# Batch 3 of a fused attention and SwiGLU kernel: its exponentials are summed on GpSimd, and its denominators are made behind the value round

## The chip, the core and the metric

The kernel runs on one core of a Trainium2 chip. The time is that of the device for one execution, in microseconds (us), as the median of three runs. In the profile PE is TensorE's matrix multiply, PEld TensorE's weight load (which runs beside it), DVE is VectorE, ACT is ScalarE, POOL is GpSimd and SP is SyncE. L258 means line 258 of the kernel.

## What is computed

There are 8 batches of 8 heads with 576 positions and 64 columns each. Attention goes through 32 memory slots: the exponentials of `phi` weigh keys and values into 32 rows for each head, and the queries attend to those rows. A SwiGLU block with 512 columns in, 1536 inside and 512 out follows.

```python
a = np.exp(phi - max(phi, axis=2))                  # (B, H, S, 32)
a = a / (np.sum(a, axis=2) + 1e-09)                 # the denominators
k_m = np.einsum('bhsm,bhsd->bhmd', a, k)
v_m = np.einsum('bhsm,bhsd->bhmd', a, v)
attn = softmax(q @ k_m^T / sqrt(64))
x = (attn @ v_m) as (B*S, 512)
g = x @ w_gate
out = (g / (1 + exp(-g)) * (x @ w_val)) @ w_out
```

The sum over the 576 positions in the second line is what the change is about.

## The kernel before

**Batches.** Batches 0 and 1 are handled together at the start. From batch 2 on, one pass of the loop at L996 handles batch b: scores, exponentials, normalisation, then "the gates" of batch b. The gates are 24 slots (`gv_slot`, L545). In each slot TensorE makes a gate product of one slot and the value product of the slot before (four matmuls of 288 columns), ScalarE takes the gate through Silu (L532), and VectorE multiplies it by the value product (L538). `spread` (L852) puts other work between the slots by keys: slot s has the key s + 0.5, and the two items of the next batch's keys and values stand at the keys 7 and 9, so behind the seventh and behind the ninth slot. Each engine runs its instructions in the order in which this program issues them.

**Keys and values of the next batch.** `kv_items(b + 1, beside)` (L292) gives two items. The first, `run_sums`, makes

- the denominators (`kv_denominators`, L239): products of 128 columns of exponentials with `ones2`, two columns wide (L258);
- the sums for keys and values (`kv_sum`, L222), 72 small matmuls (L230) into two PSUM banks;
- the reciprocal of the denominators on VectorE (L262), and `kv_norm` (L268), four VectorE instructions (L266) that scale the sums by it into `t_bkv`;
- `beside()`: the value round of the current batch's third chunk of columns (`u_item(b, 2, "aava")`), which is 16 matmuls (L472) into four banks and four copies out of them, of which the first, second and fourth are ScalarE's (L492) and the third VectorE's (L496), and then up to two units of output products of the batch before (L727). In the gates of batch 2 no such units are left.

The second item, `kv_T` (L278), transposes `t_bkv`. For batches 2 and 3 this is done on TensorE, by three products with the identity (L288), and VectorE copies the result (L289). For batches above 3 it is a DMA transpose on SyncE's queue (L284).

**Two orders of `run_sums`.** Where `phi_sum(b + 1)` has run, the exponentials of the nine row groups have been added up on GpSimd (L212), and the sum is held as two bf16 parts (L218, L219); then the batch is in `esums`, the denominators take two products, and they stand behind `beside()`, as do the reciprocal and `kv_norm`. Otherwise, with `beside` given, the denominators take nine products into a bank of their own (`p_S`) and stand first, with their reciprocal; `kv_norm` follows the sums, and `beside()` comes last. Before the change batches 4, 6 and 7 take the first way, batches 3 and 5 the second. Batch 2 is made with nothing beside it.

**GpSimd.** Its queue holds the Strassen-like sums of the hidden activations (`chunk_done`, L586, on the lines L603 and L560), the issue of the loads (L94 to L108), and `phi_sum`. That one starts with `wait_for(atts[b - 1, 1])`, a copy of one element that waits for the second normalisation (L452) of the current batch.

**PSUM.** Eight banks are handed out in the order in which they were given back in the program (`bank` and `done`, L75 to L84).

Of the kernel before, what the change touches and what calls it, by code (L numbers as in the profile page):

```python
# [14 lines left out]
def kernel(  # L15
# [98 lines left out]
    def load_qT(b):  # L114

        qTs[b] = att.tile([128, NS, 128], BF16, tag="qT", name="t_qT")
        nc.sync.dma_start_transpose(out=qTs[b], in_=qs[b])
# [52 lines left out]
    def phi_exp(b):  # L170
        t = att.tile([128, JK, NP, M], BF16, tag="ephi", name="t_ephi")
        nc.scalar.activation(
            out=t.rearrange("p j i m -> p i j m"),
            in_=phis.pop(b).rearrange("p i (j m) -> p i j m", m=M),
            func=AF.Exp,
        )
        ephis[b] = t
# [114 lines left out]
    def kv_items(b, beside=None):  # L292


        def run_sums():
            o = 2 * D
            behind = b in esums
            own = beside and not behind
            if own:
                d = bank([128, NG], FP32, "p_S")  # L300
                kv_denominators(b, d)
                kv_reciprocal(b, d)
                done(d)
            p = [bank([128, CH], FP32, f"p_kv{g}") for g in range(NG)]
            if not (own or behind):
                kv_denominators(b, p[0][:, o:o + NG])
            kv_sum(b, p, (0, 1))
            if behind:
                beside()
                kv_denominators(b, p[0][:, o:o + NG])  # L310
            if not own:
                kv_reciprocal(b, p[0][:, o:o + NG])
            kv_norm(b, p)
            if beside and not behind:
                beside()

        return [run_sums, lambda: kv_T(b)]
# [74 lines left out]
    def scores(b, g):  # L392
        p = gv_banks()
        for i in range(NP):
            for r in range(2):
                nc.tensor.matmul(  # L396
                    p[r][32 * i:32 * i + 32, 0:HALF],
                    lhsT=kTs[b][64 * r:64 * r + 64, g, 32 * i:32 * i + 32],
                    rhs=q_of(b, i, g, r),
                    start=True,  # L400
                    stop=True,
                    tile_position=(64 * r, 32 * i),
                )
        e = att.tile([128, 2, HALF], BF16, tag=f"E{g}", name="t_E")
        for r in range(2):
            scale = rks[b][:, g:g + 1] if b in rks else sm_scale
            nc.scalar.activation(
                out=e[:, r].rearrange("p (c s) -> p c s", c=NC),
                in_=p[r][:, 0:HALF].rearrange("p (s c) -> p c s", c=NC),
                func=AF.Exp,  # L410
                scale=scale,
            )
        done(*p)
        es[b, g] = e
# [35 lines left out]
    def norm(b, g):  # L450
        a = att.tile([128, 2, HALF], BF16, tag=f"A{g}", name="t_A")
        nc.vector.tensor_tensor(out=a, in0=es.pop((b, g)), in1=lzs.pop((b, g)), op=ALU.mult)  # L452
        atts[b, g] = a
# [108 lines left out]
    def weight_sums(c, part=(0, 1, 2, 3)):  # L562

        if 0 not in part:
            t = Ts[c]
            for n in part:
                x, y = Ts[c, n]
                subtract(nc.vector, t[:, n], x, y)
            return
        home = dict(tag=f"mphi{c}", bufs=1) if c < 2 else dict(tag="T2", bufs=1)  # L570
        t = att.tile([128, 4, 2, DM // 2], BF16, name="t_T", **home)
        w = WOc[c].rearrange("p (m e) f -> p e m f", e=2)
        h = DM // 2
        B11, B12, B21, B22 = (w[:, e, :, h * n:h * n + h] for e in range(2) for n in range(2))
        Ts[c] = t
        for n, xy in enumerate(((B12, B11), (B22, t[:, 0]), (B22, B12), (B21, t[:, 1]))):
            Ts[c, n] = xy
            if n in part:
                subtract(nc.vector, t[:, n], *xy)
# [62 lines left out]
    def wait_for(x):  # L642

        t = att.tile([1, 1], BF16, tag="mark", bufs=1, name="t_mark")
        nc.gpsimd.tensor_copy(out=t, in_=x)
# [183 lines left out]
    def q_items(b, evac):  # L829
        return [lambda n=n: q_T(b, n, evac[n]) for n in range(3)]  # L830
# [9 lines left out]
    def u_three(b):  # L840

        evac = "avavav" if b in (3, 5) else "avaava"
        u_round(b, (((0,), 0, (0, 1)), ((1,), 0, (0, 1)), ((0,), 1, (0, 1))), evac)

    def u_values(b):

        u_round(b, (((1,), 1, (0, 1)),), "aa")
    def run(items):
        for x in items:
            x()  # L850
# [10 lines left out]
    def exp_tables():  # L861
        nc.scalar.preload_act_table_set("natural_log_exp_and_others")
# [111 lines left out]
    def take(n):  # L974
        nonlocal backlog
        n = max(0, min(n, len(backlog)))
        part, backlog = backlog[:n], backlog[n:]
        return part
# [3 lines left out]
    def loads(b):  # L982

        if b < B:
            load_q(b)
            load_phi(b, nc.gpsimd)
            load_k(b)
            load_v(b)

    def run_late():  # L990
        run(late)
        late.clear()
# [3 lines left out]
    for b in range(2, B):  # L996
        last = b + 1 == B
        exp_tables()
        if b == 2:
            load_qT(3)  # L1000
            phi_exp(2)
            (zero, ops0), (one, ops1) = products(0, ("c11",)), products(1, ("p1", "c11"))
            kv, q2 = kv_items(2), q_items(2, "aaa")
            run(zero[:6])
            sums = {n: f for n, f in zip(((1, 1), (0, 2), (1, 2)), late)}
            late.clear()
            sums[0, 2]()
            weight_sums(0)
            weight_sums(1)
            run(zero[6:12] + one[:6] + kv[:1] + q2[:2])  # L1010
            weight_sums(2, (0, 1))
            run(zero[12:16] + zero[18:22] + kv[1:] + q2[2:] + zero[16:18] + zero[22:24])
            weight_sums(2, (2, 3))
            ops0["c11"]()
            ops1["p1"]()
            wait_for(Ts[2][0:1, 3, 0, 0:1])
            for part in ((0, 1), (3,), (2,)):
                for c in (1, 2):
                    sums[1, c](part)
            loads(4)  # L1020
            backlog = one[6:12] + zero[36:] + one[12:36]
            ops = ops1
        else:
            run(take(6))
        for g in range(NG):
            scores(b, g)
        if b > 2:
            ops["p1"]()
            u_values(b)
        else:  # L1030
            run(zero[24:36] + take(6))
        run(take(6))
        z_inv_v(b, 0)
        ops["c11"]()
        run(take(6))
        if not last:
            phi_exp(b + 1)
        z_inv_v(b, 1)
        if b > 2:
            norm(b, 0)  # L1040
            norm(b, 1)
        run(take(6))
        run_late()
        if b == 4:
            wait_for(atts[4, 1][0:1, 0, 0:1])
            quad_sums(0)
        nc.scalar.preload_act_table_set("silu_and_others")
        run(take(6))
        if b == 2:
            norm(2, 0)  # L1050
        run(take(6))
        if b == 2:
            norm(2, 1)
            u_three(2)
            run(one[36:])
        g = gv_slots(b)
        quad = []
        if b == 4:
            quad = products(b, (), 0)[0]
        if last:  # L1060
            rest, rest_ops = products(b, (), 1)
            backlog += rest[:12]
        beside = 0 if last else 2 if quad else min(4, len(backlog))
        outs = [lambda: run(take(1)) for _ in range(len(backlog) - beside)]
        streams = [(g, 0, 24), (quad[:12], 0, 3), (quad[12:], 12, 18.5)]
        streams += [(outs, 4, 7 if quad else 24)]
        if b == 2:
            streams += [([lambda: u_values(2)], 2.5, 3)]
        if last:
            streams += [([u_item(b, 2)], 5, 6)]  # L1070
        if not last:
            if b > 2:
                load_qT(b + 1)
            if b > 2 and b != 4:
                phi_sum(b + 1)
            streams += [
                (kv_items(b + 1, lambda: (u_item(b, 2, "aava")(), run(take(2)))), KV, KV + 4),
                ([lambda: (u_three(b + 1), run(take(2)))], 19, 20),
            ]
        spread(*streams)  # L1080
        flush_mul()
        units, ops = products(b, ("p1", "c11"))
        backlog += units
# [34 lines left out]
```

## Time and profile before

| what | value |
|---|---|
| median of three runs | 233.5 us (233.14 to 233.53) |
| span of the profiled execution, first to last instruction | 231.4 us |
| TensorE busy | 221.6 us, 96% |
| VectorE, ScalarE, GpSimd busy | 185.1 us (80%), 171.7 us (74%), 140.8 us (61%) |
| gates of batch 2, first to last gate product | 76.35 to 91.1 us |
| sums of batch 3 (L230) | from 80.28 us |
| transposes of batch 3 (L288) | from 82.44 us |
| granted TensorE clock, mean | 0.997 |

The page and the trace are of one execution. Its own total time is not recorded, so what lies around the span in it is not known; 2.1 us lie between the span and the median of the other runs (233.5 - 231.4). A timeline line gives the start, the duration of the merged group, the engine, the source line, the operation, what is written and read, and how many instructions are merged. For TensorE the durations of a group contain the pipeline's latency, so the distance from the start of one group to the start of the next is the time that it occupies the engine.

### The profile page before, as it was taken

To read this page: it belongs to the slowest core of one execution; us is meant where nothing else is said; L and a number is where in the kernel's file an instruction comes from. 1 tells how busy PE (TensorE), PEld (TensorE's weight loads), DVE (VectorE), ACT (ScalarE), POOL (GpSimd) and SP (SyncE) were. 2 spreads that over 40 slices of the span, in tenths; PEclk is the share of its full clock that TensorE was granted. 3 is DMA by queue.
4 is the path that set the end of the run, shared out by engine and by line. 5 is a ranking of instruction groups with operands and counts; after the bars stand their busy time and mean duration, and the time that the engine had idled before them with its cause. 6 is when DMAs were issued, how large, how long until landed. Compare 5 with 4: busy or idle time off the path is not lost.

```text
span 231.4 us, 7210 instructions
## 1 busy us (share of the span) xinstructions
PE 221.6 (96%) x2825; PEld 169.8 (73%) x2825; DVE 185.1 (80%) x423; ACT 171.7 (74%) x365; POOL 140.8 (61%) x190
## 2 busy tenths in 40 slices
PE   6987799999999999999999999999999999999993
PEld 2544476778887777878788787887788778878882
DVE  4245789999966799989997668998999899977732
ACT  2777898988447989968896658978898789677310
POOL 8422427998199049765977689464845394039291
PEclk9999999999999999999999999999999999999998
DMA  6999999999996992999299946994014502202125
GB/s 214 210 211 206 199 207 207 221 245 268 205 225 175 256 256 49 223 204 184 71 223 191 226 134 115 252 236 89 28 65 114 104 0 95 91 10 84 31 85 160
DMA packets 36674, 36.84 MB, mean 159 GB/s; under 512 B 14624, under 2 KB 31008, under 8 KB 36640
## 3 DMA queue, kind: packets, MB, share of 16 engines
q0 software_dynamic: 16272, 22.42, 52.5%
q1 hardware_dynamic: 19600, 13.18, 22.9%
q10 hardware_dynamic: 768, 0.79, 1.1%
q8 instruction: 22, 0.36, 0.6%
q14 instruction: 12, 0.10, 0.1%
HBM read 42.47 MB, written 9.44 MB: 224 GB/s over the span
## 4 chain that ended last, share of the span: by engine, by line
PE 86%; DMA 9%; POOL 2%; ACT 1%; issue 0%; DVE 0%; POOLq 0%
PE p_g L515 21%; PE p_os L727 21%; PE p_v L515 20%; PE p_oc L727 10%; DMA W<-in_moe_w_val_dram 9%; PE p_oa L727 5%; PE p_u L472 5%; PE p_kv L230 2%; PE p_g L396 1%; POOL t_kv L99 1%; POOL t_kv L103 1%; PE p_q L383 0%; POOL t_q L108 0%; ACT t_qT L337 0%; POOL W L138 0%
## 5 line engine op out<-in xcount | busy, mean ns | idle before, releaser
L538 DVE TENSOR_TENSOR t_h<-t_sg,p_v 128x288 bf16<-128x288 bf16 x192 | 81.8, 451 | 14.1 <-PE p_v L515 7.0
L515 PEld LDWEIGHTS <-t_U 128*128 128x128 bf16 x768 | 73.9, 98 | 21.2 <-issue 3.5
L532 ACT ACTIVATE t_sg<-p_g 128x288 bf16<-128x288 f32 x192 | 73.3, 424 | 17.1 <-PE p_g L515 11.4
L515 PE MATMUL p_g<-t_A,t_U 128*128 128x288 bf16 x384 | 77.0, 286 | 0.0
L515 PE MATMUL p_v<-t_A,t_U 128*128 128x288 bf16 x384 | 77.0, 286 | 0.0
L727 PEld LDWEIGHTS <-t_S 128*128 128x128 bf16 x384 | 37.5, 98 | 4.5 <-issue 0.2
L603 POOL TENSOR_TENSOR t_S<-t_h 128x512 bf16<-128x512 bf16 x17 | 19.7, 1157 | 32.7 <-DVE t_h L538 31.2
L727 PEld LDWEIGHTS <-t_h 128*128 128x128 bf16 x288 | 27.1, 98 | 8.6 <-issue 5.0
L492 ACT CAST t_U<-p_u 128x512 bf16<-128x512 f32 x51 | 27.0, 605 | 6.6 <-PE p_u L472 6.6
L727 PE MATMUL p_os<-t_T,t_S 128*128 128x256 bf16 x192 | 23.7, 273 | 0.0
L560 POOL TENSOR_TENSOR t_S<-t_S,t_h 128x512 bf16<-128x512 bf16 x17 | 19.6, 1156 | 1.3
L560 POOL TENSOR_TENSOR t_S<-t_h 128x512 bf16<-128x512 bf16 x16 | 18.4, 1152 | 0.0
L560 POOL TENSOR_TENSOR t_S<-t_h,t_S 128x512 bf16<-128x512 bf16 x16 | 18.4, 1152 | 0.0
L472 PE MATMUL p_u<-W,t_kT 64*32 64x512 bf16 (+1 forms) x416 | 15.3, 363 | 1.2 <-DMA W<-in_moe_w_gate_dram 0.6
L496 DVE CAST t_U<-p_u 128x512 bf16<-128x512 f32 x21 | 13.6, 683 | 1.9 <-PE p_u L472 1.9
L727 PE MATMUL p_os<-t_T,t_h 128*128 128x256 bf16 x96 | 14.8, 273 | 0.0
L875 PE MATMUL p_warm<-bones 128*128 128x512 bf16 x44 | 12.5, 421 | 1.7 <-DVE bones L897 1.7
L452 DVE TENSOR_TENSOR t_A<-t_E,t_lz 128x576 bf16<-128x576 bf16 x16 | 11.4, 740 | 0.7 <-ACT t_lz L428 0.7
L727 PE MATMUL p_oc<-t_T,t_S 128*128 128x256 bf16 x96 | 11.9, 273 | 0.0
L727 PE MATMUL p_oa<-WO,t_h 128*128 128x256 bf16 x96 | 11.8, 273 | 0.0
L727 PE MATMUL p_oc<-WO,t_S 128*128 128x256 bf16 x96 | 11.8, 272 | 0.1
L727 PE MATMUL p_os<-WO,t_h 128*128 128x256 bf16 x96 | 11.8, 273 | 0.0
(107 smaller groups left out, 308.3 us busy)
## 6 DMA issues: line engine op xcount, KB each, us to landing
out_dram<-t_o SPq DMA_DIRECT2D x11, 512.0 KB, 3.0
t_kv<-in_k_dram POOLq DMA_DIRECT2D x8, 576.0 KB, 10.5
t_q<-in_q_dram POOLq DMA_DIRECT2D x8, 576.0 KB, 8.4
t_kv<-in_v_dram POOLq DMA_DIRECT2D x8, 576.0 KB, 14.7
t_phi<-in_phi_dram POOLq DMA_DIRECT2D x6, 576.0 KB, 8.1
out_dram<-t_o SPq DMA_DIRECT2D x10, 256.0 KB, 4.5
WO<-in_moe_w_out_dram POOLq DMA_DIRECT2D x3, 512.0 KB, 19.2
W<-in_moe_w_gate_dram POOLq DMA_DIRECT2D x2, 512.0 KB, 16.5
```

Of the source, the lines that this page charges most:

```text
L230: nc.tensor.matmul(p[g][32 * i:32 * i + 32, 0:n], lhsT=phi_of(b, g, j, i), rhs=kvs[b][64 * g:64 * g + 64, w0:w1, i, j * D:(j + 1) * D], st ...
L452: nc.vector.tensor_tensor(out=a, in0=es.pop((b, g)), in1=lzs.pop((b, g)), op=ALU.mult)
L472: nc.tensor.matmul(p[g][32 * i:32 * i + 32, o:o + n], lhsT=kTs[b][64 * g:64 * g + 64, 2, 32 * i:32 * i + 32], rhs=w_part(w, c, i, g, halve ...
L492: nc.scalar.copy(out=t, in_=p)
L496: nc.vector.tensor_copy(out=t, in_=p)
L515: nc.tensor.matmul(p[:, 0:HALF], lhsT=Us[b, c, g][:, o // 2, which, 128 * (o % 2):128 * (o % 2 + 1)], rhs=atts[b, g][:, r], start=(g == 0) ...
L532: nc.scalar.activation(out=sg, in_=gate[:, 0:HALF], func=AF.Silu)
L538: nc.vector.tensor_tensor(out=dst, in0=sg, in1=val[:, 0:HALF], op=ALU.mult)
L560: eng.tensor_tensor(out=out, in0=x, in1=y, op=ALU.subtract)
L603: eng.tensor_tensor(out=t[:, 0], in0=A21, in1=A22, op=ALU.add)
L727: nc.tensor.matmul(mine[home][:, u], lhsT=lhs(c, m, u), rhs=rhs(c, m), start=fresh and u == 0, stop=(k == 5), skip_group_check=u == 1 or n ...
L875: nc.tensor.matmul(p[:, 0:128 * a], lhsT=bones, rhs=x.to_broadcast([128, a, 128]) if a > 1 else bones, start=True, stop=True,)
```

## The change

`phi_sum(b + 1)` is called for b = 2 too. So the nine groups of exponentials of batch 3 are added on GpSimd, ahead of all that its queue gets from the gates of batch 2, and `run_sums` of batch 3 takes the other of its two orders. Nothing else is edited.

```diff
         if not last:
             if b > 2:
                 load_qT(b + 1)
-            if b > 2 and b != 4:
+            if b != 4:
                 phi_sum(b + 1)
             streams += [
                 (kv_items(b + 1, lambda: (u_item(b, 2, "aava")(), run(take(2)))), KV, KV + 4),
```

For batch 3 the program then issues, in this order: on GpSimd the wait, four additions, a cast and a subtraction; in the gates of batch 2, behind the seventh slot, the sums (L230), the value round with its four copies, two denominator products, the reciprocal, and the four instructions of `kv_norm`; two slots later `kv_T`. The nine products into `p_S` and that bank are gone.

## The prediction, made before the result was seen

> **What bounds the kernel now.** I read the page first, then the chain of waits, then stretches of time, then the timeline of the place. In the page TensorE is the only engine near the full span:
>
> ```profile
> PE 221.6 (96%) x2825; PEld 169.8 (73%) x2825; DVE 185.1 (80%) x423; ACT 171.7 (74%) x365; POOL 140.8 (61%) x190
> PE 86%; DMA 9%; POOL 2%; ACT 1%; issue 0%; DVE 0%; POOLq 0%
> ```
>
> The 9% of DMA belong to the first weights, long before the place of the change. The stretches around it (length, then busy time and instructions of PE, PEld, DVE, ACT, POOL, then the clock, DMA share, GB/s) show TensorE full, VectorE nearly so, and GpSimd empty until 82.6:
>
> ```profile
> 76.00:80.00 4.00, 4.00 (x40) 2.90 (x39) 2.56 (x7) 4.00 (x12) 0.00 (x0) 1.00 0.99 268
> 80.00:82.60 2.60, 2.60 (x110) 1.94 (x108) 2.30 (x9) 1.65 (x5) 0.00 (x0) 1.00 1.13 277
> 82.60:88.00 5.40, 5.40 (x48) 4.22 (x44) 5.03 (x14) 4.80 (x14) 4.08 (x4) 1.00 1.17 238
> ```
>
> From 70 us to its last product, some 227 us, the chain in order of time is almost all TensorE, one product behind another. So what TensorE loses at 80 us is lost at the end, and what it saves is saved. The question is what its queue does here. Timeline of batch 3 as it is now:
>
> ```profile
> 79.73 0.41 PE L515 MATMUL p_v<-t_A,t_U 128*128 128x288 bf16 x2
> 79.98 0.37 PE L258 MATMUL p_S<-ones,t_ephi 128*128 128x2 bf16 x9
> 80.28 0.80 PE L230 MATMUL p_kv<-t_kv,t_ephi 64*32 64x128 bf16 x72
> 80.86 0.66 PE L472 MATMUL p_u<-W,t_kT 64*32 64x512 bf16 x16
> 81.12 0.99 DVE L266 TENSOR_SCALAR t_bkv<-p_kv,t_rS 128x128 bf16<-128x128 f32 x4 [0.30 <-PE p_kv L230]
> 81.45 0.42 PE L515 MATMUL p_g<-t_A,t_U 128*128 128x288 bf16 x2
> 82.03 0.68 DVE L496 CAST t_U<-p_u 128x512 bf16<-128x512 f32 x1
> 82.32 0.28 PEld L288 LDWEIGHTS <-t_bkv 128*128 128x128 bf16 x3
> 82.44 0.33 PE L288 MATMUL p_T<-ident,t_bkv 128*128 128x128 bf16 x3
> 82.61 0.41 PE L515 MATMUL p_g<-t_A,t_U 128*128 128x288 bf16 x2
> ```
>
> The normalisation ends at 81.12 + 0.99 = 82.11, and TensorE comes to the transposes that need it at 82.44 without a stop. The margin is small, 0.2 us to the first weight load at 82.32. Batch 4 is already made in the new order, and it is the model for each new step:
>
> ```profile
> 102.57 0.41 PE L515 MATMUL p_v<-t_A,t_U 128*128 128x288 bf16 x2
> 102.91 0.80 PE L230 MATMUL p_kv<-t_kv,t_ephi 64*32 64x128 bf16 x72
> 103.50 0.66 PE L472 MATMUL p_u<-W,t_kT 64*32 64x512 bf16 x16
> 104.19 0.69 DVE L496 CAST t_U<-p_u 128x512 bf16<-128x512 f32 x1 [0.64 <-PE p_u L472]
> 104.53 0.19 PE L258 MATMUL p_kv<-ones,t_ehl 128*128 128x2 bf16 x2
> 104.59 0.41 PE L515 MATMUL p_g<-t_A,t_U 128*128 128x288 bf16 x2
> 104.79 0.16 DVE L262 RECIPROCAL t_rS<-p_kv 128x2 f32<-128x2 f32 x1
> 104.99 0.99 DVE L266 TENSOR_SCALAR t_bkv<-p_kv,t_rS 128x128 bf16<-128x128 f32 x4
> ```
>
> One thing differs. Batch 4's transposes are a DMA's, and TensorE does not wait there. Batch 3's are TensorE's own, two slots on, in an in-order queue.
>
> **Part 1: the sum on GpSimd.** In batch 4 the waiting copy starts at 99.54 and the last subtraction ends at 103.11 + 0.43 = 103.54: 4.0 us for seven instructions. For batch 3 the wait is for the normalisation that VectorE runs from 74.90 for 0.75 us; GpSimd has issued its last load by 74.34 + 0.76 = 75.10. With the 0.12 us from that normalisation's end to the copy (batch 4: 99.42 to 99.54), it starts at 75.77 and ends at 79.77. The products that read it come at 81.25 (part 3), 1.5 us later. No DMA is issued by the step. Queued behind it are the sums of batch 2's first chunk, which start at 83.84 after an idle time:
>
> ```profile
> 74.34 0.76 POOL L103 DMA_DIRECT2D t_kv<-in_v_dram  x1
> 83.84 1.15 POOL L603 TENSOR_TENSOR t_S<-t_h 128x512 bf16<-128x512 bf16 x1 [8.75 <-DVE t_h L538]
> ```
>
> So the cost is nothing, covered by those 8.75 us of idle time; without that cover the 4.0 us would delay those sums, and the four loads behind them at 91.47 to 94.3. SyncE's queue is not touched.
>
> VectorE runs beside it. In batch 4's stretch, with the sum running, its six gate multiplications take 455 ns on average; in the eleven of 84 to 88.5, without it, 450. Four or five fall under the new sum: 0.03 us, in a stretch where VectorE waits 0.73, 0.38 and 0.33 us for ScalarE. I take 0. The Trainium skill ("GPSIMD Engine Reference", section 1, Specifications) says that GpSimd shares its SBUF interfaces with VectorE and contends with VectorE instructions that read two SBUF inputs. That speaks against this change in general; here the one such instruction, the normalisation, is over when the sum starts, and the casts and multiplications beside it read PSUM. By the rule as by the row the sum below stays as it is; were the contention there, only the 1.5 us of margin would shrink.
>
> **Part 2: TensorE's products.** Removed: nine, 79.98 to 80.28 = 0.30 us, but this holds the change of array tiling to the small matmuls, which remains. From a value product to the sums directly it takes 102.91 - 102.57 = 0.34 us, against 0.25 between products of the slots: 0.09 for the change of tiling. Added: two, 104.59 - 104.53 = 0.06. Sum: -0.30 + 0.09 + 0.06 = **-0.15 us**.
>
> **Part 3: the order behind them.** The sums start at 79.73 + 0.34 = 80.07, the value round 0.59 later at 80.66, the two denominators 0.59 later at 81.25, the slots go on at 81.31. Banks do not hold this up: without `p_S` the sums take banks that are free earlier in the rotation. Two slots of four products at 0.245 us a pair bring TensorE to the transposes at 81.31 + 0.98 = 82.29.
>
> VectorE now runs the cast of the value round first. In batch 4 that starts 0.69 after the round (104.19 - 103.50), the reciprocal 0.60 later, the four scalings 0.20 later still, for 0.99. For batch 3: cast 80.66 + 0.69 = 81.35, reciprocal 81.95 (its operand is there at 81.25 + 0.19 = 81.44, so the cast ahead of it decides), scalings 82.15 to **83.14**. From VectorE's end to a weight load that waits for it, a copy of the start-up ends at 19.93 and the load starts at 19.98: 0.05; from weight load to transposes 0.12 (82.32, 82.44). So the transposes start at 83.31 instead of being reached at 82.29: a stop of **1.02 us**. Behind them in TensorE's queue are all later slots. Within the stop there is a smaller one: the second slot's value product takes the bank of ScalarE's second copy, free at 80.66 + 0.47 + 2 x 0.52 = 82.2 instead of 82.04; it comes before the same wait and adds nothing.
>
> After it the transposes take 0.17 and the slots go on at 83.48, against 82.61 before: **+0.87 us** = 1.02 - 0.15. VectorE then multiplies for two waiting slots (83.06 to 83.94), copies the transposes, and is at the next multiplication at 84.2, which is when its value product is done; from there it needs 0.435 us a slot to TensorE's 0.49, so nothing more is carried. Behind that TensorE is full to the end, so all 0.87 reach the end: span 231.44 + 0.87 = 232.3, and with the 2.1 us by which the runs' median lies over the profiled span, 233.5 + 0.87 = **234.4 us**.
>
> Bounds: the trace has no waiting transpose behind a DVE scaling. If the cast started as early as ScalarE's copy of the first half (0.47 after the round, not 0.69), the stop is 0.8, net +0.65; if nothing of the two slots fits in before it (value product held until 82.3 and the rest behind), or 0.3 of VectorE's lateness comes back at the six-bank round at 88, net +1.2. With 0.2 for the scatter of medians that gives 233.9 to 234.9.
>
> **The rivals.**
> - *No stop: only the saving.* The transposes find their operand, as they do now. The place is the weight load at 82.17 (82.29 - 0.12); it decides if the scalings end by 82.12, a whole 1.02 earlier than I have them. For it: the margin exists today. Against it: VectorE runs in program order, and cast (0.60), reciprocal (0.20) and scalings (0.99) already make 1.79 after 81.35. Price -0.15: 233.35, no change that can be told. Chance 0.08.
> - *Half a stop.* The time is partly given back later, at a wait that TensorE has anyway. For it: weight loads show 10.5 us of waits from 50 us on (lines L727, L472, L515, L396, L230). Against it: the starts of products in the chain are evenly spaced from 82 to 92 us, so there is nothing to give it back to. Net +0.4: 233.9. Chance 0.07.
> - *The sum is late.* It needs GpSimd to run past 81.7 (from 81.25, plus the 0.44 that VectorE's cast covers). If its additions took twice as long, 8.0 us, it ends at 83.77, and then the denominators, two slots (1.04) and the stop for scalings: operand 83.96, reciprocal 84.03, scalings 84.23 to 85.22, transposes 85.39, slots on at 85.56: +2.95, 236.4. Against it: all three sums in the trace take 4.0 us, batch 4's beside a VectorE that is busier (3.84 of 4.1 us, here 2.76 of 4.2). Chance 0.03.
> - *The branch is not taken.* The test for `esums` is made when `run_sums` runs, behind `phi_sum`; so it is. Time as before with an idle sum, 233.5. Chance 0.01.
> - *Something unforeseen gains.* At most the nine products could go, 0.30 us. Chance 0.02 for faster.
>
> **How the numbers follow.** The forecast (a stop of about 1 us, time 233.9 to 234.9) has 0.79. What a measurement of this kernel can tell from no change is about 0.2%, 0.47 us. Slower by more than that: nearly all of the forecast, the late sum and half of the half stop, 0.85. Within: no stop, the other half, the branch and a little of the forecast, 0.13. Faster: 0.02. The range reaches down to a small net loss and up to 1.5 us: 233.6 to 235.0.
>
> **What would show it.** Right: in the changed trace a wait of the weight load of `t_bkv` (L288) on VectorE's L266 of about 1 us near 83.2; the sum over on GpSimd before 80; the sums (L230) at 80.07; slots going on near 83.5; the shift of 0.87 constant from there to the end. Wrong: transposes at 82.3 with no wait, a shift that shrinks between 84 and 100, or a denominator product that waits for GpSimd.

## The result, and the profile after

| kernel | median, us | runs | span of the profiled execution, us |
|---|---|---|---|
| before | 233.53 | 15 | 231.4 |
| changed | 234.12 (233.91 to 234.46) | 15 | 232.1 |

The ratio is 1.0025, with a 95% interval of 1.0016 to 1.0034: the change costs 0.6 us (0.37 to 0.79). In the page of the changed kernel the busy times hardly differ from those of before, though the kernel is slower:

```profile
PE 222.9 (96%) x2818; PEld 169.9 (73%) x2818; DVE 185.3 (80%) x423; ACT 171.7 (74%) x365; POOL 144.3 (62%) x197
```

TensorE has seven instructions less and GpSimd seven more, with 3.5 us of work. TensorE's 1.3 us more of busy time lie in the first 27 us (21.05 before, 22.36 changed), far ahead of the change; from 76 to 92 us it is busy for 15.36 us instead of 16.00. In the chain that ended last the cast, the reciprocal and the scalings on VectorE now stand between 81.25 and 83.06 us, where before there were only products of TensorE. The timeline of TensorE and VectorE at the place of the change, in the changed kernel:

```profile
79.57 0.41 PE L515 MATMUL p_v<-t_A,t_U 128*128 128x288 bf16 x2
79.91 0.80 PE L230 MATMUL p_kv<-t_kv,t_ephi 64*32 64x128 bf16 x72
80.49 0.66 PE L472 MATMUL p_u<-W,t_kT 64*32 64x512 bf16 x16
81.08 0.20 PE L258 MATMUL p_kv<-ones,t_ehl 128*128 128x2 bf16 x2
81.15 0.41 PE L515 MATMUL p_g<-t_A,t_U 128*128 128x288 bf16 x2
81.25 0.69 DVE L496 CAST t_U<-p_u 128x512 bf16<-128x512 f32 x1 [0.67 <-PE p_u L472]
81.66 0.41 PE L515 MATMUL p_g<-t_A,t_U 128*128 128x288 bf16 x2
81.86 0.16 DVE L262 RECIPROCAL t_rS<-p_kv 128x2 f32<-128x2 f32 x1
82.05 0.99 DVE L266 TENSOR_SCALAR t_bkv<-p_kv,t_rS 128x128 bf16<-128x128 f32 x4
82.14 0.41 PE L515 MATMUL p_v<-t_A,t_U 128*128 128x288 bf16 x2
83.10 0.17 PEld L288 LDWEIGHTS <-t_bkv 128*128 128x128 bf16 x3 [0.86 <-DVE t_bkv L266]
83.11 0.34 PE L288 MATMUL p_T<-ident,t_bkv 128*128 128x128 bf16 x3 [0.56 <-DVE t_bkv L266]
83.28 0.41 PE L515 MATMUL p_g<-t_A,t_U 128*128 128x288 bf16 x2
88.77 0.84 PE L472 MATMUL p_u<-W,t_kT 64*32 64x512 bf16 x24
227.47 0.81 PE L727 MATMUL p_os<-t_T,t_x 128*128 128x256 bf16 x6
```

The same two ends in the kernel before:

```profile
88.09 0.84 PE L472 MATMUL p_u<-W,t_kT 64*32 64x512 bf16 x24
226.78 0.81 PE L727 MATMUL p_os<-t_T,t_x 128*128 128x256 bf16 x6
```

Read the starts down TensorE's lines. From the last value product (79.57) to the next gate product (81.15) it takes 1.58 us; before, it took 1.72 (79.73 to 81.45). That is the saving of the seven products. Then come two slots, and the products of L288 stand until 83.11: their weight load waited 0.86 us for VectorE's L266, which ends at 82.05 + 0.99 = 83.04. There is a smaller gap ahead of it, at 82.14: the second slot's value product starts 0.48 us after its gate product (81.66) instead of 0.24.

A duration in brackets understates the wait, because the model of a matmul's end contains the pipeline's latency (0.56 us at the product, 0.86 at its weight load). The starts are the better ruler, so I measure each run by one **stretch** on TensorE: from the last value product ahead of the sums to the six-bank round, the 24 products of L472 (88.77 above). I split it at the first gate product behind the denominators or the value round, here 81.15. The first part holds the products that the change edits, the second the waits.

The stretch takes 8.36 us before (1.72 + 6.64) and 9.20 changed (1.58 + 7.62): 0.14 saved and 0.98 lost, together **+0.84 us**. Nothing of it is given back behind it: from the six-bank round to the last group of output products it is 138.69 us before (88.09 to 226.78) and 138.70 changed (88.77 to 227.47). In the traces of the runs below it is 138.69 to 138.75, and 139.01 in the second trace of the changed kernel, so it is never shorter than before. The changed execution came to the place 0.16 us earlier; its first gate products start at 27.04 us instead of 27.20, behind the first weights' DMA. That is scatter of the start: over all ten traces the last value product ahead of the sums starts between 79.57 and 79.80 us. It is why the spans differ by 0.7 and not by 0.84.

The profiled execution of the changed kernel took 233.91 us, the lowest of its 15. In every run listed with its span, the time is 1.7 to 1.9 us longer than the span, so the 2.1 us between the span and the median of before hold about 0.3 us by which that execution was quicker than the median (an estimate from these spans).

GpSimd's part, in the changed kernel's timeline of that engine:

```profile
79.11 0.43 POOL L219 TENSOR_TENSOR t_ehl<-t_es,t_ehl 128x128 bf16<-128x128 f32 x1
83.85 1.16 POOL L603 TENSOR_TENSOR t_S<-t_h 128x512 bf16<-128x512 bf16 x1 [4.31 <-DVE t_h L538]
```

The sum starts at 75.55 and is over at 79.11 + 0.43 = 79.54, 1.54 us before the first product that reads it (81.08), and the next work on GpSimd still comes after 4.31 us of idle time.

### The profile page after: what moved, and what is told of

Its sections match the earlier page's. It is cut to its first block, busy times and chain, and to the rows that moved or that the text cites. A ratio compares the mean times of both kernels' runs of the same rounds, so it can differ in the third digit from the quotient of the medians.

```text
span 232.1 us, 7204 instructions
## 1 busy us (share of the span) xinstructions
PE 222.9 (96%) x2818; PEld 169.9 (73%) x2818; DVE 185.3 (80%) x423; ACT 171.7 (74%) x365; POOL 144.3 (62%) x197
## 4 chain that ended last, share of the span: by engine, by line
PE 85%; DMA 9%; POOL 2%; DVE 1%; issue 1%; ACT 1%; POOLq 0%; DVEq 0%
PE p_os L727 21%; PE p_g L515 21%; PE p_v L515 20%; PE p_oc L727 10%; DMA W<-in_moe_w_val_dram 9%; PE p_oa L727 5%; PE p_u L472 5%; PE p_kv L230 2%; PE p_g L396 1%; POOL t_kv L99 1%; POOL t_kv L103 1%; PE p_q L383 0%; POOL t_q L108 0%; ACT t_qT L337 0%; POOL W L138 0%
## 5 line engine op out<-in xcount | busy, mean ns | idle before, releaser
L472 PE MATMUL p_u<-W,t_kT 64*32 64x512 bf16 (+1 forms) x416 | 15.3, 363 | 1.0 <-DMA W<-in_moe_w_val_dram 0.9
L875 PE MATMUL p_warm<-bones 128*128 128x512 bf16 x44 | 13.8, 457 | 1.7 <-DVE bones L897 1.7
```

The source lines that it names most:

```text
L472: nc.tensor.matmul(p[g][32 * i:32 * i + 32, o:o + n], lhsT=kTs[b][64 * g:64 * g + 64, 2, 32 * i:32 * i + 32], rhs=w_part(w, c, i, g, halve ...
L875: nc.tensor.matmul(p[:, 0:128 * a], lhsT=bones, rhs=x.to_broadcast([128, a, 128]) if a > 1 else bones, start=True, stop=True,)
```

## The experiments

The theory is that the loss is TensorE's wait at its own transposes, because the new order makes the denominators behind the value round and puts the cast of that round ahead of the reciprocal on VectorE's queue. The rivals are that GpSimd's work disturbs something, that the products in their new place cost by themselves, and that part of the loss is given back later. All times are ratios to the kernel before, with runs of both on one chip. The table has TensorE's stretch in two parts, as above.

| run | products | rest | stretch, us | ratio (95%) |
|---|---|---|---|---|
| before | 1.72 | 6.64 | 8.36 | 1 |
| changed | 1.58 | 7.62 | 9.20 | 1.0025 (1.0016 to 1.0034) |
| changed, again | 1.58 | 7.61 | 9.19 | 1.0037 (1.0023 to 1.0051) |
| scalings ahead of the value round | 1.76 | 6.71 | 8.47 | 0.9998 (0.9989 to 1.0006) |
| sum made and not read | 1.72 | 6.64 | 8.36 | 0.9995 (0.9980 to 1.0011) |
| transposes one slot later | 1.58 | 7.12 | 8.70 | 1.0011 (1.0001 to 1.0022) |
| transposes two slots later | 1.58 | 6.88 | 8.46 | 0.9999 (0.9991 to 1.0008) |
| transposes by DMA | 1.58 | 8.75 | 10.33 | 1.0137 (1.0099 to 1.0175) |
| VectorE copies second | 1.58 | 7.43 | 9.01 | 1.0022 (1.0012 to 1.0032) |
| two products in the place of the nine | 1.55 | 6.64 | 8.19 | 0.9986 (0.9977 to 0.9994) |

**GpSimd's sum alone.**

```diff
-        esums[b] = hl
+        if b != 3:
+            esums[b] = hl
```

> GpSimd sums the exponentials of batch 3 in the gates of batch 2 as in the change, but nothing reads the sum: the denominators take the nine products in the old place. Theory: GpSimd's work is covered, stretch 8.36 us as before, time that of before within 0.1 us. Rival (GpSimd's 4 us disturb VectorE or later loads): stretch above 8.5, or time 0.3 us or more over before.

The stretch is that of before to the hundredth, and so is the time (233.19 beside 233.32 us). The work on GpSimd costs nothing that the trace shows, and by the interval not more than 0.26 us. That rival is out as the source of the 0.84 us.

**Scalings ahead of the value round.** For batch 3 the denominators, reciprocal and scalings come before `beside()`:

```diff
             if behind:
-                beside()
+                if b != 3:
+                    beside()
                 kv_denominators(b, p[0][:, o:o + NG])
...
-            if beside and not behind:
+            if beside and (not behind or b == 3):
                 beside()
```

> The sum on GpSimd and the two denominator products stay, but for batch 3 the denominators, the reciprocal and the four scalings are issued ahead of the value round. Measured by the stretch on TensorE from the last value product ahead of the sums (L230) to the first product of the six-bank round (L472, 24 products): 8.36 us before, 9.20 changed. Theory (the loss is TensorE's wait at the transposes, because VectorE has the cast of the value round ahead of the reciprocal): no wait at L288, stretch 8.36 - 0.15 = 8.2 us, time 0.1 to 0.2 us under the kernel before. Rival (the sum on GpSimd or the products behind the sums cost by themselves): the stretch stays at 9.0 or more, time 0.5 us over before.

The wait is gone, as the theory has it (rest 6.71 beside 7.62 us), and with it the loss in the time: 233.26 beside 233.32 us. But the stretch was to be 8.2 and is 8.47. Of the 0.26 too much, 0.19 are in the products and 0.07 at the second slot's value product, which starts at 82.29, 0.31 us behind its gate product (81.98) instead of 0.24. Timeline of this run, whose lines behind the edit are numbered one higher:

```profile
79.72 0.41 PE L516 MATMUL p_v<-t_A,t_U 128*128 128x288 bf16 x2
80.06 0.80 PE L230 MATMUL p_kv<-t_kv,t_ephi 64*32 64x128 bf16 x72
80.79 0.20 PE L258 MATMUL p_kv<-ones,t_ehl 128*128 128x2 bf16 x2
80.92 0.63 PE L473 MATMUL p_u<-W,t_kT 64*32 64x512 bf16 x16
81.48 0.42 PE L516 MATMUL p_g<-t_A,t_U 128*128 128x288 bf16 x2
82.29 0.42 PE L516 MATMUL p_v<-t_A,t_U 128*128 128x288 bf16 x2
```

The two denominator products use the whole array (128\*128) and now stand between two groups in tiles of 64\*32. The sums take 0.73 us to the next start instead of 0.58, and the two products 0.13 instead of 0.07; the value round takes 0.03 less. The block is 1.76 - 1.58 = 0.18 us longer, for two more changes between these tilings; the two do not cost the same, 0.09 is only their mean. That is more than the 0.14 us that the change saves there. The Trainium skill ("TensorEngine Tiling (Array Packing)", section Tiling Modes, Key Properties) says that a change of the tiling mode drains TensorE, without a price; the two more of this run took 0.18 us together.

**Transposes later.** The two items of `kv_items` are put at the keys 7 and 10, and at 7 and 11, instead of 7 and 9:

```diff
-                (kv_items(...), KV, KV + 4),
+                (kv_items(...), *((KV - 0.5, KV + 5.5) if b == 2 else (KV, KV + 4))),
```

One slot later:

> As changed, with batch 3's transposes three slots behind the value round (two as changed, four in the run with two slots more). Theory (wait = the scalings' end less the time at which TensorE reaches the transposes): one slot more is 0.49 us less of waiting, stretch 9.20 - 0.49 = 8.71 us, and a wait of about 0.25 is left at L288 (with four slots it was gone and the stretch 8.46). Rival (the wait follows something that is not covered by slots): stretch 9.0 or more.

Two slots later (`KV - 1, KV + 7`):

> As changed, but the transposes of batch 3 (L288) stand four slots behind the value round instead of two. Theory in its simple form (only the distance from scalings to transposes counts): the 0.98 us of two slots cover the wait of 0.98, stretch 8.2 to 8.3 us, time at or 0.1 under before. Second form (the banks that the value round and the scalings give back later hold TensorE too: 0.24 us at the second slot's value product in the changed trace, and perhaps 0.2 at the next gate): no wait at L288, but the stretch is 8.5 to 8.6 and the time 0.2 over before. Rival (not the transposes): 9.0 or more.

With two, three and four slots between value round and transposes the rest of the stretch is 0.98, 0.48 and 0.24 us over that of before. The first step is one slot's 0.49 us, as expected; the second only 0.24. With four slots nothing waits at L288 any more (it starts at 83.59, 0.24 us behind the value product ahead of it), and what is left is the small gap at the second slot's value product, here 0.49 us behind its gate product instead of 0.24:

```profile
81.88 0.41 PE L515 MATMUL p_g<-t_A,t_U 128*128 128x288 bf16 x2
82.37 0.40 PE L515 MATMUL p_v<-t_A,t_U 128*128 128x288 bf16 x2
```

So the second form of that expectation holds in kind, a little too high in size (8.5 to 8.6 expected, 8.46 found, time equal to before). The further 0.2 at the next gate did not come.

**VectorE copies second.** In the gates of batch 2 VectorE takes the second copy of the value round, not the third:

```diff
-u_item(b, 2, "aava")
+u_item(b, 2, "avaa" if b == 2 else "aava")
```

> As changed, but of the value round's four copies in the gates of batch 2 VectorE takes the second instead of the third. That copy can start 0.25 to 0.3 us earlier, and the bank that held the second slot's value product comes free with it. Theory (the cast ahead of the reciprocal on VectorE's queue sets the end of the scalings): reciprocal, scalings and transposes 0.2 to 0.28 earlier, stretch 8.9 to 9.0; no wait at the second slot's value product, but that gives nothing while the transposes wait. Rival (the denominator products or the GpSimd sum set the reciprocal): stretch stays 9.2.

Timeline of this run:

```profile
81.12 0.69 DVE L496 CAST t_U<-p_u 128x512 bf16<-128x512 f32 x1 [0.49 <-PE p_u L472]
```

The cast starts 1.50 us behind the last value product (81.12 and 79.62) instead of 1.68 (81.25 and 79.57), and the stretch is shorter by the same, 9.20 - 9.01 = 0.19 us. The direction is as expected, the size at the low end of it, because the cast starts only 0.18 earlier and not 0.25 to 0.3. The small gap is gone (gate 81.71, value 81.95), and gives nothing here. So the end of the cast does set the time of the reciprocal and with it the wait, and the small gap follows from the order of the copies.

The cast is not the whole of the wait, though. In the changed kernel the denominators are there at 81.08 + 0.20 = 81.28. With the 0.04 us from there to a reciprocal that has no cast ahead of it (80.99 to 81.03 in the run with the scalings first), the scalings would end at 82.50 and the transposes start at 82.57, still 0.44 us behind the 82.13 at which TensorE would reach them. By this estimate the cast makes 0.54 us of the 0.98, and the late place of the denominators the rest. No run separates the two.

**Transposes by DMA.**

```diff
-        if b > 3:
+        if b > 2:
             nc.sync.dma_start_transpose(...)
```

> As changed, but batch 3's transposes are made by a DMA on SyncE's queue, as those of batches 4 to 7 are; TensorE's three products and VectorE's copy of them go. Theory: TensorE waits for no scaling any more; stretch 8.36 - 0.15 - 0.17 = 8.0 us if the banks do not hold it, 8.3 if the 0.24 us at the second slot's value product stays; time 0.1 to 0.3 under before. If the DMA lands after 88 us the six-bank round waits for it, and the stretch is longer by that. Rival (not the transposes): 9.0 or more.

A miss in the time: 2.5 us slower than before by the medians, 2.3 to 4.1 by the interval. The wait at TensorE's own transposes goes, and the one that the expectation named as its condition comes. Timeline of this run:

```profile
87.69 0.41 PE L515 MATMUL p_v<-t_A,t_U 128*128 128x288 bf16 x2
90.06 0.84 PE L472 MATMUL p_u<-W,t_kT 64*32 64x512 bf16 x24 [1.96 <-DMA t_kT<-t_bkv]
```

Up to 87.69 all is as expected: with the usual 0.34 to the six-bank round it would have been 8.30 us. But the transposes land 6.7 us after their issue at 83.28, at about 90.0, and the round stands for 2.03 us. The stretch is 1.97 us longer than before; what the time has above that (two of the six runs took 238 us) this trace does not explain. In the kernel before, the DMA transposes of batches 4 to 7 land 3.8, 5.0, 2.3 and 2.6 us after their issue, and their six-bank rounds start 4.4, 6.7, 5.5 and 5.5 us after it, so none waits. Here the round would have come 4.75 us after the issue, which is more than batch 4 has: it is the slower landing that costs, not a shorter time. Why this one is slower is open. Between issue and landing the busy share of the 16 DMA engines is full for both (the view gives 1.18 for the 4.75 us here and 1.13 for batch 4's 3.8 us), with 235 GB/s moved here and 124 there.

**Two products in the place of the nine.** The sum is used, but the order stays that of before:

```diff
-            behind = b in esums
+            behind = b in esums and b != 3
```

> The sum on GpSimd is used, but in the old order: the two denominator products stand ahead of the sums, in a bank of their own, in the place of the nine, and value round, copies and scalings are in the order of before. Theory: seven products of 23 ns go, with no further change of tiling and no wait: stretch 8.36 - 0.16 = 8.20 us, time 0.1 to 0.2 under before; GpSimd's sum must be over by 79.8, and in the changed trace it is over at 79.54. Rival (the products in any place that waits for GpSimd cost): a wait at L258 and a stretch above 8.36.

Timeline of this run:

```profile
79.73 0.41 PE L515 MATMUL p_v<-t_A,t_U 128*128 128x288 bf16 x2
79.98 0.19 PE L258 MATMUL p_S<-ones,t_ehl 128*128 128x2 bf16 x2
80.10 0.80 PE L230 MATMUL p_kv<-t_kv,t_ephi 64*32 64x128 bf16 x72
87.92 0.84 PE L472 MATMUL p_u<-W,t_kT 64*32 64x512 bf16 x24
```

Nothing waits: the products start 0.25 behind the last value product and hand over to the sums 0.12 later, where the nine took 0.30. The stretch is 8.19 us as expected. The time is 232.97 beside 233.38 us, and the interval lies below 1: this version is the fastest of all here. Its gain by the medians, 0.4 us, is larger than the 0.17 of the stretch; the interval (0.14 to 0.54 us) holds both. It was measured once.

**The changed kernel again.**

> The changed kernel itself, beside the kernel before on the same chip, for the size: the trace's stretch from the last value product ahead of the sums to the six-bank round grew by 0.84 us (8.36 to 9.20), the medians by 0.59. If all of the 0.84 reaches the end, the time is 0.8 over before and the interval holds 1.0036; if part is given back behind the stretch, it is 0.5 to 0.6 again.

The ratio is 1.0037, so 0.54 to 1.19 us, and the stretch 9.19. The whole 0.84 lies in this interval and 0.05 us above that of the first series; about 0.8 (1.0034) is the upper edge of the first interval and lies inside the second. As the time from the six-bank round to the end is in no trace shorter than before, I read the smaller first median as scatter, of which the start (0.16 us between two traces) is one part. This is argued from the traces; no run takes the start away.

**Left open.** Two things were not measured: the changed order with both waits removed at once (transposes two slots later and VectorE copying second), for which a stretch of 8.2 to 8.25 us was expected, and the version with two products in the place of the nine a second time. For the first, an estimate from the table is 8.46 - 0.24 = 8.22 us, if the two gains add up.

## Why the prediction was right

The forecast was 234.4 us, +0.87; the stretch gives +0.84, the two series of medians +0.6 and +0.8. The +0.87 lies a little above the interval of the first series (0.37 to 0.79) and inside that of the second (0.54 to 1.19). Step by step, with the trace's times moved by the 0.16 us by which the changed execution came earlier:

| step | predicted, us | in the trace |
|---|---|---|
| GpSimd's sum, start and end | 75.77, 79.77 | 75.71, 79.70 |
| sums (L230) | 80.07 | 80.07 |
| value round, then denominators | 80.66, 81.25 | 80.65, 81.24 |
| slots go on | 81.31 | 81.31 |
| VectorE's cast, reciprocal | 81.35, 81.95 | 81.41, 82.02 |
| scalings end | 83.14 | 83.20 |
| transposes start | 83.31 | 83.27 |
| slots go on | 83.48 | 83.44 |

- *The bound.* TensorE's order decided, and what it lost at 83 us is lost at the end. Right, by the 138.69 and 138.70 us, which no later trace undercuts.
- *GpSimd at no cost.* Right within 0.26 us, shown by the run with the sum made and not read.
- *The products at -0.15.* Right: -0.14. That it held the change of tiling apart from the nine products was what made it right; the run with the scalings first, with two more such changes, took 0.18 us more.
- *The stop of 1.02.* Right in kind, 0.98 in size. The term that was most off is the 0.12 us from weight load to product, taken from a row where TensorE was busy: where it stands, the product follows its weight load by 0.01 (83.10, 83.11). VectorE's chain was 0.06 later than its model in batch 4, which makes up for half of that.
- *The small stop at the second slot's value product.* Right in place and in that it adds nothing to this kernel; 0.24 us, where the prediction had 0.16. Where the transposes come later it is what remains.
- *The rivals.* "No stop" and "half a stop" fall by the wait of 0.86 us in the trace and the equal times behind it; "the sum is late" by 1.54 us of margin; "the branch is not taken" by the two products in the nine's place.

What the prediction did not ask is whether the saving can be had without the new order. It can: the run with two products in the place of the nine, measured once, keeps 0.17 us of it in the stretch, so the loss comes only from the order that `esums` brings with it.

## What to carry to other kernels

A path that suits one stage need not suit another: here TensorE waits nowhere for the late denominators of batch 4, whose result a DMA transposes (its six-bank round follows the slots' last product by the usual 0.34 us), while those of batch 3 cost 1 us where the bounding engine transposes it itself two slots later. When an edit puts work ahead of an instruction on a side engine, follow that queue to the next instruction of the bounding engine that reads its result, and compare the two arrival times; the margin of 0.2 us was legible in the trace of before. If the saving is worth having, take it without the new order.

## What the runs showed of the hardware

- From a value product in 128\*128 to the sums in 64\*32 TensorE took 0.34 us, against 0.25 from product to product within the slots: 0.09 us more. Two more changes between these tilings in one run took 0.18 us together, more than the 0.14 us that seven products less had saved.
- A DMA transpose of 128 x 384 bf16 from one on-chip tile to another took 6.7 us to land at 83 us, and 2.3 to 5.0 us in the other batches. A full share of the DMA engines alone does not tell them apart: it was 1.18 with 6.7 us, and 1.13 with batch 4's 3.8 us.
- A weight load that had waited for VectorE started 0.06 us after VectorE's end (83.04, 83.10), and its product 0.01 after the load's start.
